# Gate order in the prelude, choice of PSUM banks and load times of the filter slices in a spectral + GeGLU kernel

## Chip, cores and metric

The kernel runs on one core of one Trainium2 chip. The metric is device time in microseconds (us) of one execution, as the median over repeated runs. Five engines work side by side, each through its own queue of instructions in order: TensorE (PE; its weight loads are shown apart as PEld), VectorE (DVE), ScalarE (ACT), GpSimd (POOL) and SyncE (SP). SP, ACT and POOL also issue DMA transfers. Engines wait for each other by semaphores.

## What is computed

The input is layer-normalised, goes through a global spectral filter (two-dimensional real FFT over sequence and features, product with a complex weight, inverse FFT) and through a gated feed-forward layer; both results are added to the input. Sizes: sequence 2048, features 512, feed-forward 1792, bf16 in and out.

```python
xn = _layernorm(x, axis=-1)
# A: spectral filter
X = rfft2(xn.astype(float32), axes=(-2, -1))          # 2048 x 257
y = irfft2(X * (w_r + 1j * w_i), s=(S, D)).astype(bfloat16)
# B: gated feed-forward
h = gelu(xn @ w_gate) * (xn @ w_up)                    # 2048 x 1792
return x + y + h @ w_down
```

## The kernel before

The 2048 rows are 16 row tiles of 128, grouped into 4 blocks `b` of 4 tiles. `xnT` holds the normalised input transposed, so that each 128-row tile is the moving operand of the feed-forward matmuls.

**Feed-forward.** For each block and each of 14 slices `fc` of 128 hidden columns, `gate(b, fc)` runs 4 matmuls on PE (L880) into one PSUM bank, ScalarE applies GELU from the bank into one of three buffers `gl` (L883); `up(b, fc)` runs 4 matmuls (L895) into another bank and VectorE multiplies the two into `hT` (L901). The product with `w_down` is made in a Strassen-like scheme on 7 matmul groups per pair of row tiles: `product(b, p, step)` (L784), with sums of `hT` from VectorE (`sum_01`, L719; `sums_S`, L701) and of `w_down` (`sums_T`, L746). Step 0 is copied between its two banks by ScalarE (L803), and step 1 adds to that copy. Step 2 is the first to read the sums.

**Spectral filter.** It is a chain of small DFT stages on PE, each emptied by ScalarE: a butterfly on VectorE over `xnT` (`butter`, L438 and L439, then L441 and L442), `unit_D` (L455 to L459, evicted by L463), `units_A` (L487 and L490, evicted by L497, then stored to the scratch `scr1` by SP), a reload of the scratch into `tv` (`load_tv`, two loads per block on SP), `unit_B` (L587, evicted by L593, then multiplied on VectorE by the filter slices `wring`, L598), `unit_C` (L612, evicted by L617, stored to `scr2`), `load_vv`, `unit_E` (L640, evicted by L647) and `unit_F` (L838, evicted by L844, then combined and added into the result by a DMA). `unit_B(0)` reads all of `tv`, that is, the loads of all four blocks.

**Layer norm and transposes.** VectorE makes the statistics (`ln_stat`, L385) and the normalised rows (`ln_norm`, L404). Blocks 0 and 1 are transposed on PE (`trans1`, `trans`, L1021 and L414); blocks 2 and 3 by one transposing DMA each on SP's queue (`trans_dma`, L428).

**Order of the work.** Everything is written out by the program in one order; each engine's queue is what that order leaves to it. It begins with a prelude (L1032 to L1061): 12 matmuls on zeros, layer norm of the first tiles one by one, and gates and ups of slices 0 to 5 for the first two tiles of block 0 alone (`T01`), since the first two tiles arrive first. Gates and ups before the main loop may be issued with `ahead`, the number of gates that were issued already and whose `up` isn't yet, so that `gl` buffers aren't mixed up. Then the main loop runs over blocks and slices: gate, `hook()`, up, `hook()`, with products in between. Each `hook()` is a numbered slot; `at(h, ...)` plans calls into slot `h`, in the order in which they were planned. So `at` places the filter chain, the statistics of later blocks and late loads among the feed-forward work.

The slots that matter here: `butter(m, 0)` and `butter(m, 1)` stand in slots `t + 2` and `t + 3` of block `m`'s `t` (L966); `units_A(2)` and `unit_D(12)` in slot 40, `unit_D(13)` to `(15)` in slots 41 to 43; `load_tv(3)` in 48; `sum_01(0, 0, k)` in the slots of L1007; `sums_T(k)` in those of L1009; `unit_B(0)` in 59, `unit_B(1)` in 63, `unit_C(0)` in 64. Slot 28 is the first of block 1.

**Filter slices.** `load_W(s)` makes 8 loads of 64 KB for slice `s`: four of `w_r` on POOL's queue in slots `h0` and `h0 + 1`, then four of `w_i` on SP's queue in `h0 + 2` and `h0 + 3`. `load_late` holds a load back until PE has come to the point of the program where it was planned. The buffer `wring` holds four slices. `keep_256(s)` is a small copy on POOL that waits for slice `s` and must come before slice `s + 4` overwrites it.

**PSUM banks.** There are 8 banks. `take(n, dur, hold)` picks `n` neighbouring banks for the next piece of PE work. It carries a planned PE time `pt`, a planned ScalarE time `act_t` and for each bank the planned time `free` at which it is empty again, and takes the place whose banks are free first; of equals, the lowest:

```python
i = min(range(9 - n), key=lambda i: max(free[i:i + n]))
```

Stages A, B, C and the products take pairs. The plan only chooses the bank; the real order is kept by semaphores, so a PE instruction waits until the bank's last reader is done.

Of the kernel before, what the change touches and what calls it, by code (L numbers as in the profile page):

```python
# [18 lines left out]
P = 128  # L19
# [112 lines left out]
class _Prog:  # L132
# [17 lines left out]
    def op(self, eng, fn, r=(), w=(), dma=False, after=()):  # L150
        deps = [(ev, True) for ev in after]
        for k in r:
            if k in self.writer:
                deps.append((self.writer[k], True))
        for k in w:
            if k in self.writer:
                deps.append((self.writer[k], False))
            for ev in self.readers.get(k, ()):
                deps.append((ev, False))
        need = {}  # L160
        for (st, val), raw in deps:
            if st == eng and not dma and (eng == "pe" or not raw):
                continue
            need[st] = max(need.get(st, 0), val)
        known = self.known[eng]
        need = {s: v for s, v in need.items() if known.get(s, 0) < v}
        need = {s: v for s, v in need.items()
                if not any(s2 != s and self.clk[(s2, v2)].get(s, 0) >= v for s2, v2 in need.items())}
        for s, v in need.items():
            for a, b in self.clk[(s, v)].items():  # L170
                if known.get(a, 0) < b:
                    known[a] = b
        if dma:

            st = None if eng == "pool" else next((d for d in self.dsem if known.get(d, 0) >= self.cnt[d]), None)
            if st is None:
                st = "d%d" % (len(self.sem) - 4)
                self.sem[st] = self.es.enter_context(self.nc.semaphore("s_" + st))
                self.cnt[st] = 0
                if eng != "pool":  # L180
                    self.dsem.append(st)
            self.cnt[st] += 16
            ev, inc = (st, self.cnt[st]), 16
            clk = dict(known)
        else:
            self.cnt[eng] += 1
            ev, inc = (eng, self.cnt[eng]), 1
            clk = dict(self.lastclk[eng])
            for a, b in known.items():
                if clk.get(a, 0) < b:  # L190
                    clk[a] = b
        clk[ev[0]] = ev[1]
        self.clk[ev] = clk
        if not dma:
            self.lastclk[eng] = clk
        self.q[eng].append((fn, list(need.items()), ev[0], inc))
        for k in r:
            self.readers.setdefault(k, []).append(ev)
        for k in w:
            self.writer[k] = ev  # L200
            self.readers[k] = []
        return ev
# [12 lines left out]
def bass_parallel_sum__spectral_gfnet__glu_gated_geglu__prompt_kernel(  # L215
# [27 lines left out]
    with ExitStack() as es:  # L243
        def sb(name, shape, dt):
            return es.enter_context(nc.sbuf_tensor(name, shape, dt))

        pr = _Prog(nc, es)
        op = pr.op

        x_sb = sb("x_sb", [P, NJ, D], BF16)  # L250
        xnT = sb("xnT", [P, NJ, 4, P], F16)
# [5 lines left out]
        wg_sb = sb("wg", [P, 4, FF], BF16)  # L257
# [54 lines left out]
        def bank(i):  # L312
            return psum[:, i * 512:(i + 1) * 512]
# [7 lines left out]
        pt = [0.0]  # L321
        act_t = [0.0]
        free = [0.0] * 8

        def take(n, dur, hold=None, ops=1):
            i = min(range(9 - n), key=lambda i: max(free[i:i + n]))
            pt[0] += dur
            if hold is None:
                act_t[0] = max(act_t[0], pt[0] + 0.25) + 0.2 + 0.43 * n
                end = act_t[0]  # L330
            else:
                end = pt[0] + hold
            for k in range(i, i + n):
                free[k] = end
            return i
# [48 lines left out]
        def ln_stat(j):  # L384
            op("dve", lambda e: e.bn_stats(st[:, j, :], x_sb[:, j, :]), r=[("x", j, 0), ("x", j, 1)], w=[("st", j)])  # L385
# [482 lines left out]

        gun = [0]

        def gate(b, fc, jjs=(0, 1, 2, 3), ahead=0):
            k = gun[0] + ahead
            n = len(jjs) * P
            j0 = 4 * b + jjs[0]
            bg = take(1, 0.0017 * n)

            def fn(e):
                ins = None
                for dc in range(4):
                    ins = e.matmul(bank(bg)[:, 0:n], wg_sb[:, dc, fc * P:(fc + 1) * P], xnT[:, j0:j0 + len(jjs), dc, :], start=(dc == 0), stop=(dc == 3))  # L880
                return ins
            op("pe", fn, r=[("wg", fc)] + [("xnT", b, dc, jj) for dc in range(4) for jj in jjs], w=[("ps", bg)])
            op("act", lambda e: e.activation(gl[k % 3][:, 0:n], bank(bg)[:, 0:n], ACT.Gelu_apprx_tanh), r=[("ps", bg)], w=[("gl", k % 3)])  # L883

        def up(b, fc, jjs=(0, 1, 2, 3), wait=False):
# [49 lines left out]
        def at(h, *calls):  # L935
            plan.setdefault(int(h), []).extend(calls)
# [14 lines left out]
            at(10 + 2 * i, (load_late, wd_sb[:, f0:f1, :], wdv[:, f0:f1, :], [("wd", fc) for fc in range(f0, f1)]))  # L951
        at(18, (load_late, be[:], c_be.ap(), ["be"]))
        at(19, (load_late, mm[:], c_mm.ap(), ["mm"]))
        for s, h0 in enumerate((24, 31, 37, 53, 61, 66, 70, 75)):
            for i, t in enumerate(load_W(s)):
                at(h0 + i // 2, t)
            at(89 + s // 2 if s > 3 else (47, 48, 51, 58)[s], (keep_256, s))
        cmv = c_cm.ap().rearrange("p (h r c) -> p h r c", h=NJ, r=2)
        for i, h0 in enumerate((54, 57, 63, 68)):
            hs = slice(4 * i, 4 * i + 4)  # L960
# [2 lines left out]
        for m in range(1, 4):  # L963
            a = (5, 15, 22)[m - 1]
            n = (10, 20, 27)[m - 1]
            t = (16, 29, 36)[m - 1]  # L966
            for i in range(4):
                at(a + i, (ln_stat, 4 * m + i))
            at(a + 3, (ln_aggr, 4 * m, 4))
            for i in range(4):  # L970
                at(n + i // 2, (ln_norm, 4 * m + i))
            if m < 2:
                at(t, (trans, m, (0, 1), (0, 1, 2, 3)))
                at(t + 1, (trans, m, (2, 3), (0, 1, 2, 3), "act"))
            else:
                at(n + 1, (trans_dma, m))
            at(t + 2, (butter, m, 0))
            at(t + 3, (butter, m, 1))
        at(3, (butter, 0, 0))
        at(4, (butter, 0, 1))  # L980
        for m in range(4):
            h = (11, 22, 35, 40)[m]
# [6 lines left out]
        for g in range(9):  # L989
            h = int(59 + 4.6 * g)  # L990
# [13 lines left out]
            at(107 + 2.2 * j, (unit_E, j))  # L1004
            at(110.5 + 2.2 * j, (unit_F, j))
        for k in range(3):
            at((36, 37, 38)[k], (sum_01, 0, 0, k))  # L1007
        for k in range(4):
            at((39, 43, 45, 47)[k], (sums_T, k))  # L1009
        for k in range(4):  # L1010
            at((101, 101, 102, 103)[k], (sums_S, 2, 0, 4, (k,)))
            at((106, 106, 107, 107)[k], (sums_S, 2, 4, 6, (k,)))
# [27 lines left out]
        ln_norm(1)  # L1040
        trans1(1, ("dve", "act"))
        T01 = (0, 1)
        gate(0, 0, T01)
        ln_stat(2)
        ln_stat(3)
        ln_aggr(2, 2)
        up(0, 0, T01)
        gate(0, 1, T01)
        up(0, 1, T01)
        gate(0, 2, T01)  # L1050
        ln_norm(2)
        ln_norm(3)
        up(0, 2, T01)
        gate(0, 3, T01)
        gate(0, 4, T01, 1)
        up(0, 3, T01)
        up(0, 4, T01)
        trans(0, (0, 1), (2, 3), "dve")
        trans(0, (2, 3), (2, 3), "act")
        gate(0, 5, T01)  # L1060
        up(0, 5, T01)  # L1061
        S3 = {7: [(0, 4, (0,))], 8: [(0, 4, (1,))], 9: [(0, 4, (2,))], 10: [(0, 4, (3,))], 11: [(4, 6, (0, 1))], 12: [(4, 6, (2, 3))],
              13: [(6, 7, (0, 1, 2, 3))]}
# [3 lines left out]
        for b in range(4):  # L1067
            for n, fc in enumerate(range(NFC) if b < 2 else [7 * (i % 2) + i // 2 for i in range(NFC)]):
                jjs = (2, 3) if b == 0 and fc < NH else (0, 1, 2, 3)
# [70 lines left out]
```

## Time and profile before

| | us |
|---|---|
| median of 11 runs | 182.17 (181.15 to 185.1) |
| the profiled execution | 183.22 |
| its span, first to last instruction | 181.4 |

Groups of instructions with most busy time, by line:

| line | engine | what | count | busy us | mean ns |
|---|---|---|---|---|---|
| L880 | PE | gate | 248 | 58.4 | 359 |
| L895 | PE | up | 248 | 58.4 | 359 |
| L901 | DVE | product of gate and up | 62 | 39.3 | 637 |
| L883 | ACT | GELU | 62 | 34.4 | 556 |
| L784 | PE | product with wd, hT | 112 | 14.4 | 273 |
| L598 | DVE | filter product | 16 | 10.3 | 687 |

Matmuls are pipelined, so the mean of one is longer than its distance to the next: four gate matmuls of 512 columns take 0.86 us in a row on the chain of waits. DMA moved 27.89 MB, 154 GB/s in the mean over the span; the mean busy share of the 16 DMA engines, in 40 slices of the span, in tenths:

```profile
DMA  3999999699999566488763121384155755642104
```

A row of a timeline gives the start in us from the span's start, the duration, engine, line, operation, output and inputs, count, and in brackets how long the engine sat idle before it and which instruction released it. "A waits" rows give total, times and longest. SPq and POOLq stand for the issue of DMAs.

### The profile page before, as it was taken

To read this page: it belongs to the slowest core of one execution; us is meant where nothing else is said; L and a number is where in the kernel's file an instruction comes from. 1 tells how busy PE (TensorE), PEld (TensorE's weight loads), DVE (VectorE), ACT (ScalarE), POOL (GpSimd) and SP (SyncE) were. 2 spreads that over 40 slices of the span, in tenths; PEclk is the share of its full clock that TensorE was granted. 3 is DMA by queue.
4 is the path that set the end of the run, shared out by engine and by line. 5 is a ranking of instruction groups with operands and counts; after the bars stand their busy time and mean duration, and the time that the engine had idled before them with its cause. 6 is when DMAs were issued, how large, how long until landed. Compare 5 with 4: busy or idle time off the path is not lost.

```text
span 181.4 us, 3822 instructions
## 1 busy us (share of the span) xinstructions
PE 172.8 (95%) x1406; PEld 108.2 (60%) x1406; DVE 132.8 (73%) x331; ACT 94.0 (52%) x158; POOL 53.5 (29%) x107
## 2 busy tenths in 40 slices
PE   7879999999987999999999999999999999999992
PEld 2468655554546566556655556556676767666882
DVE  3486989987665776776876649797877777897552
ACT  3335547765576632465655755336858677632110
POOL 2210081373250206276470000001354625640000
PEclk9999999999999999999999999999999999999999
DMA  3999999699999566488763121384155755642104
GB/s 97 308 261 305 318 264 317 179 205 186 255 185 155 152 177 175 103 187 192 221 174 90 58 61 58 109 245 171 20 98 105 130 114 102 106 73 43 33 2 116
DMA packets 31059, 27.89 MB, mean 154 GB/s; under 512 B 7120, under 2 KB 27984, under 8 KB 30912
## 3 DMA queue, kind: packets, MB, share of 16 engines
q1 hardware_dynamic: 26016, 19.88, 45.0%
q0 software_dynamic: 4272, 7.24, 18.6%
q10 hardware_dynamic: 752, 0.52, 1.1%
q8 instruction: 11, 0.18, 0.4%
q14 instruction: 8, 0.07, 0.1%
HBM read 18.19 MB, written 6.29 MB: 135 GB/s over the span
## 4 chain that ended last, share of the span: by engine, by line
PE 80%; DMA 8%; DVE 6%; SPq 2%; issue 2%; ACT 1%; DVEq 0%
PE ps L784 24%; PE ps L895 23%; PE ps L880 22%; DMA wu<-in_B_w_up_dram 4%; DMA xnT<-cmx 4%; SPq L338 2%; PE ps L612 2%; PE ps L838 2%; PE ps L640 2%; PE ps L587 2%; DVE st L385 1%; DVE hT L901 1%; DVE cmx L404 1%; PE ps L458 1%; PE ps L459 1%
## 5 line engine op out<-in xcount | busy, mean ns | idle before, releaser
L895 PE MATMUL ps<-xnT,wu 128*128 128x512 f16 (+1 forms) x248 | 58.4, 359 | 1.1 <-DMA wu<-in_B_w_up_dram 1.1
L880 PE MATMUL ps<-xnT,wg 128*128 128x512 f16 (+1 forms) x248 | 58.4, 359 | 0.5 <-ACT xnT L1030 0.5
L901 DVE TENSOR_TENSOR hT<-ps,gl 128x512 bf16<-128x512 f32 (+1 forms) x62 | 39.3, 637 | 21.7 <-PE ps L895 15.4
L883 ACT ACTIVATE gl<-ps 128x512 bf16<-128x512 f32 (+1 forms) x62 | 34.4, 556 | 37.5 <-PE ps L880 34.9
L895 PEld LDWEIGHTS ps<-xnT,wu 128*128 128x128 bf16 x248 | 23.3, 98 | 20.6 <-DMA wu<-in_B_w_up_dram 1.3
L880 PEld LDWEIGHTS ps<-xnT,wg 128*128 128x128 bf16 x248 | 23.3, 98 | 16.1 <-issue 1.4
L341 POOL DMA_DIRECT2D wring<-in_A_w_r_dram x32 | 18.5, 609 | 22.6 <-PE ps L784 9.4
L649 POOL COPY tv<-tv 1x128 bf16<-1x128 bf16 x16 | 5.4, 340 | 42.0 <-ACT tv L647 41.9
L784 PE MATMUL ps<-wd,hT 128*128 128x256 bf16 x112 | 14.4, 273 | 0.0
L864 POOL DMA_DIRECT2D x_sb<-tv x16 | 13.2, 865 | 3.4 <-DVE tv L857 2.4
L385 DVE BATCH_NORM_STATS2 st<-x_sb 128x6 f32<-128x512 bf16 x16 | 10.6, 685 | 3.9 <-DMA x_sb<-in_A_x_dram 3.9
L598 DVE TENSOR_TENSOR early<-early,wring 128x1024 bf16<-128x1024 f16 x16 | 10.3, 687 | 3.8 <-ACT early L593 3.8
L803 ACT ACTIVATE ps<-ps 128x256 f32<-128x256 f32 x16 | 5.9, 369 | 13.1 <-PE ps L784 13.0
L463 ACT ACTIVATE early<-ps 128x512 f16<-128x512 f32 x16 | 9.5, 596 | 5.4 <-PE ps L459 5.4
L784 PEld LDWEIGHTS ps<-wd,hT 128*128 128x128 bf16 x112 | 10.7, 98 | 2.5
L784 PE MATMUL ps<-arena,xnT 128*128 128x256 f16 x91 | 11.4, 273 | 0.0
L844 ACT ACTIVATE tv<-ps 128x512 bf16<-128x512 f32 x16 | 9.5, 595 | 3.6 <-PE ps L838 3.6
L393 POOL TENSOR_TENSOR rstd<-vpe,mhalf 128x4 f32<-128x4 f32 (+2 forms) x6 | 5.0, 837 | 21.5 <-DVE vpe L392 21.5
L647 ACT ACTIVATE tv<-ps 128x512 bf16<-128x512 f32 x16 | 9.5, 596 | 3.2 <-PE ps L640 3.2
L593 ACT ACTIVATE early<-ps 128x1024 f16<-128x1024 f32 x8 | 8.2, 1023 | 4.8 <-PE ps L587 4.8
L784 PEld LDWEIGHTS ps<-arena,xnT 128*128 128x128 f16 x91 | 8.5, 98 | 2.3 <-DVE tw L807 0.3
L667 DVE TENSOR_TENSOR x_sb<-ps,x_sb 128x256 bf16<-128x256 f32 x16 | 6.7, 421 | 3.3 <-PE ps L784 3.2
(119 smaller groups left out, 235.7 us busy)
## 6 DMA issues: line engine op xcount, KB each, us to landing
wring<-in_A_w_r_dram POOLq DMA_DIRECT2D x32, 64.2 KB, 3.6
wring<-in_A_w_i_dram SPq DMA_DIRECT2D x32, 64.2 KB, 3.9
tv<-scr SPq DMA_DIRECT2D x8, 256.0 KB, 4.7
scr<-early SPq DMA_DIRECT2D x8, 256.0 KB, 2.2
wring<-scr SPq DMA_DIRECT2D x4, 512.0 KB, 7.9
x_sb<-tv POOLq DMA_DIRECT2D x16, 128.0 KB, 2.7
scr<-early SPq DMA_DIRECT2D x15, 128.0 KB, 3.6
out_dram<-x_sb SPq DMA_DIRECT2D x28, 64.0 KB, 2.0
```

What stands on the lines that cost most here:

```text
L341: op(eng, lambda e: e.dma_start(dst, src), w=list(keys) + list(also), dma=True, after=[("pe", pr.cnt["pe"])])
L385: op("dve", lambda e: e.bn_stats(st[:, j, :], x_sb[:, j, :]), r=[("x", j, 0), ("x", j, 1)], w=[("st", j)])
L463: op("act", lambda e: e.activation(x4.rearrange("p (a c r) -> p a c r", a=2, r=4), bank(bk).rearrange("p (a r c) -> p a c r", a=2, r=4), A ...
L598: op("dve", lambda e, k=k: e.tensor_tensor(pp[i][k], xc[i], W[k][g % 4][:, :, :, 0:256], ALU.mult), r=[("xc", i)] + [key for c in range(2) ...
L647: op("act", lambda e: e.activation(z, bank(bk).rearrange("p (a c) -> p a c", a=4), ACT.Copy, scale=SC_E), r=[("ps", bk)], w=[zk] + (TVK if ...
L784: ins = e.matmul(o, st_(f), mv(f), start=(f == 0 and step in (0, 5)), stop=(f == 6), skip_group_check=True)
L844: op("act", lambda e: e.activation(o2, bank(bk), ACT.Copy), r=[("ps", bk)], w=[ok] + (TVK if j < 2 else []))
L864: op("pool", lambda e: e.dma_start(x_sb[:, j, :], ys, accum_op=ALU.add), r=[yk + (0,), yk + (1,), ("x", j, 0), ("x", j, 1)] + acc(j), w=ac ...
L880: ins = e.matmul(bank(bg)[:, 0:n], wg_sb[:, dc, fc * P:(fc + 1) * P], xnT[:, j0:j0 + len(jjs), dc, :], start=(dc == 0), stop=(dc == 3))
L883: op("act", lambda e: e.activation(gl[k % 3][:, 0:n], bank(bg)[:, 0:n], ACT.Gelu_apprx_tanh), r=[("ps", bg)], w=[("gl", k % 3)])
L895: ins = e.matmul(bank(bu)[:, 0:n], wu_sb[:, dc, fc * P:(fc + 1) * P], xnT[:, j0:j0 + len(jjs), dc, :], start=(dc == 0), stop=(dc == 3))
L901: op("dve", lambda e: e.tensor_tensor(hT[b % 2][:, fc, h0:h0 + n], bank(bu)[:, 0:n], gl[k % 3][:, 0:n], ALU.mult), r=[("ps", bu), ("gl", k ...
```

## The change

Five edits, with no change to what is computed.

1. In the prelude, the first gate is issued tile by tile: eight matmuls of 128 columns in two groups that each need one tile's `xnT`, into the same bank, evicted by one ScalarE operation as before.
2. The prelude's order: gates 0, 1, 2 are issued ahead of ups 0, 1, 2, and gates 3, 4, 5 ahead of up 3; the transposes of tiles 2 and 3 (`trans`) come after up 3 instead of after up 4.
3. `take` ranks places by three numbers in turn: how long until the place's banks are free, counted from now; how soon two neighbouring pairs that don't overlap would be free if this place were taken; and the old number.
4. Filter slices: `load_W(0)`, `(1)`, `(2)`, `(3)` start in slots 30, 37, 49, 54 instead of 24, 31, 37, 53; `keep_256(2)` in slot 57 instead of 51.
5. Block 3's `t` is 35 instead of 36, so its butterfly stands in slots 37 and 38 instead of 38 and 39; `sum_01(0, 0, k)` in slots 38, 39, 40 instead of 36, 37, 38, and `sums_T(0)` in 40 instead of 39.

```diff
         def take(n, dur, hold=None, ops=1):
-            i = min(range(9 - n), key=lambda i: max(free[i:i + n]))
+            def cost(i):
+
+                fr = [max(0.0, f - pt[0]) for f in free]
+                own = max(fr[i:i + n])
+                fr[i:i + n] = [own + 1.5] * n
+                ps = [max(fr[k:k + 2]) for k in range(7)]
+                return own, min(ps[k] + ps[m] for k in range(5) for m in range(k + 2, 7)), max(free[i:i + n])
+
+            i = min(range(9 - n), key=cost)
...
-        def gate(b, fc, jjs=(0, 1, 2, 3), ahead=0):
+        def gate(b, fc, jjs=(0, 1, 2, 3), ahead=0, split=False):
             k = gun[0] + ahead
             n = len(jjs) * P
-            j0 = 4 * b + jjs[0]
             bg = take(1, 0.0017 * n)
 
-            def fn(e):
-                ins = None
-                for dc in range(4):
-                    ins = e.matmul(bank(bg)[:, 0:n], wg_sb[:, dc, fc * P:(fc + 1) * P], xnT[:, j0:j0 + len(jjs), dc, :], start=(dc == 0), stop=(dc == 3))
-                return ins
-            op("pe", fn, r=[("wg", fc)] + [("xnT", b, dc, jj) for dc in range(4) for jj in jjs], w=[("ps", bg)])
+            for h in (jjs,) if not split else [(jj,) for jj in jjs]:
+                j1, c = 4 * b + h[0], slice(P * (h[0] - jjs[0]), P * (h[-1] - jjs[0]) + P)
+
+                def fn(e, h=h, j1=j1, c=c):
+                    ins = None
+                    for dc in range(4):
+                        ins = e.matmul(bank(bg)[:, c], wg_sb[:, dc, fc * P:(fc + 1) * P], xnT[:, j1:j1 + len(h), dc, :], start=(dc == 0), stop=(dc == 3),
+                                       skip_group_check=split)
+                    return ins
+                op("pe", fn, r=[("wg", fc)] + [("xnT", b, dc, jj) for dc in range(4) for jj in h], w=[("ps", bg)])
             op("act", lambda e: e.activation(gl[k % 3][:, 0:n], bank(bg)[:, 0:n], ACT.Gelu_apprx_tanh), r=[("ps", bg)], w=[("gl", k % 3)])
...
-        for s, h0 in enumerate((24, 31, 37, 53, 61, 66, 70, 75)):
+        for s, h0 in enumerate((30, 37, 49, 54, 61, 66, 70, 75)):
             for i, t in enumerate(load_W(s)):
                 at(h0 + i // 2, t)
-            at(89 + s // 2 if s > 3 else (47, 48, 51, 58)[s], (keep_256, s))
+            at(89 + s // 2 if s > 3 else (47, 48, 57, 58)[s], (keep_256, s))
...
-            t = (16, 29, 36)[m - 1]
+            t = (16, 29, 35)[m - 1]
...
         for k in range(3):
-            at((36, 37, 38)[k], (sum_01, 0, 0, k))
+            at((38, 39, 40)[k], (sum_01, 0, 0, k))
         for k in range(4):
-            at((39, 43, 45, 47)[k], (sums_T, k))
+            at((40, 43, 45, 47)[k], (sums_T, k))
...
         T01 = (0, 1)
-        gate(0, 0, T01)
+        gate(0, 0, T01, 0, True)
+        gate(0, 1, T01, 1)
+        gate(0, 2, T01, 2)
         ln_stat(2)
         ln_stat(3)
         ln_aggr(2, 2)
         up(0, 0, T01)
-        gate(0, 1, T01)
         up(0, 1, T01)
-        gate(0, 2, T01)
+        up(0, 2, T01)
         ln_norm(2)
         ln_norm(3)
-        up(0, 2, T01)
         gate(0, 3, T01)
         gate(0, 4, T01, 1)
+        gate(0, 5, T01, 2)
         up(0, 3, T01)
-        up(0, 4, T01)
         trans(0, (0, 1), (2, 3), "dve")
         trans(0, (2, 3), (2, 3), "act")
-        gate(0, 5, T01)
+        up(0, 4, T01)
         up(0, 5, T01)
```

On the engines, the number of matmuls grows by four (1406 to 1410, the split gate's), with the same columns; all other counts stay. On VectorE the butterfly of block 3 moves ahead of the three `sum_01`. On SP, the four `w_i` loads of slice 0 move from ahead of the second transposing DMA to behind it, and slice 2's four from ahead of the stores of `units_A(2)` to behind `load_tv(3)`. On POOL, slice 0 moves behind the last layer-norm operation, and slice 2 behind the first two `keep_256`.

## The prediction

> **What bounds the kernel now.** I read the page first (busy time, slices, granted clock), then TensorE's waits, then the order of time around each wait, last the DMA issues. The page:
>
> ```profile
> span 181.4 us, 3822 instructions
> PE 172.8 (95%) x1406; PEld 108.2 (60%) x1406; DVE 132.8 (73%) x331; ACT 94.0 (52%) x158; POOL 53.5 (29%) x107
> PEclk9999999999999999999999999999999999999999
> ```
>
> TensorE (PE) is busy 95% of the span at the full granted clock, and the change neither adds nor removes a column of matmul work. So it can win only where PE stands still, and lose only where it makes PE stand still. PE's waits (total, times, longest):
>
> ```profile
> PE ps L455 <- DVE arena L442: 1.7, 1, 1.7
> PE ps L380 <- DVE dumm L350: 1.2, 1, 1.2
> PE ps L895 <- DMA wu<-in_B_w_up_dram: 1.1, 1, 1.1
> PE ps L880 <- ACT xnT L1030: 0.5, 1, 0.5
> PE ps L612 <- ACT early L593: 0.3, 1, 0.3
> ```
>
> Apart from the launch wait (L380) that is 3.6 us, 2% of the span: the ceiling. About 3 us after PE's last matmul are untouched. The longest wait, in order of time:
>
> ```profile
> 45.24 2.99 SPq L428 DMA_TRANSPOSE xnT<-cmx  x1
> ...
> 52.15 0.69 DVE L438 TENSOR_TENSOR cmx<-xnT 128x1024 f16<-128x1024 f16 x1 [1.37 <-DMA xnT<-cmx]
> ...
> 53.36 0.69 DVE L719 TENSOR_TENSOR xnT<-hT 128x512 f16<-128x512 bf16 x2
> 53.97 0.68 DVE L901 TENSOR_TENSOR hT<-ps,gl 128x512 bf16<-128x512 f32 x1
> 54.57 0.41 DVE L441 TENSOR_TENSOR arena<-cmx 128x512 f16<-128x512 f16 x1
> 54.90 0.42 DVE L442 TENSOR_TENSOR arena<-cmx 128x512 f16<-128x512 f16 x1
> ...
> 55.38 0.23 PE L455 MATMUL ps<-fd,arena 128*128 128x128 f16 x1 [1.69 <-DVE arena L442]
> ```
>
> The reader should see two causes: the transposing DMA of the last row block is issued at 45.24 and lands 6.9 us later (its median in the DMA table), and VectorE then puts three other operations between the butterfly's halves (L439, L441).
>
> **Part by part** (minus is time gained).
>
> *Prelude.* `up` of slice 3 waits until 12.31 for the second slice of `w_up`, whose place in SP's queue is unchanged. Before, gates 0 to 4 stand ahead of that wait; after, gates 0 to 5. Moved out from behind it: four 128x256 matmuls, 0.44 on the chain: **-0.44**. The transposes now follow one `up` (0.44) after 12.31 instead of two, at 12.75; their inputs (L404) ended at 12.25, and one product more (0.38) now precedes them on VectorE: 12.63, still in time. ScalarE evicts gates 3 to 5 while PE waits. Bounds: 0 if `w_up` lands later by as much, -0.6 if the 0.07 gap behind goes too.
> Tile by tile, gate 0 is eight matmuls of 128 columns instead of four of 256. The 128-column transposes (L414) take 0.45 for eight, so 0.44 stays 0.44; the first half starts up to 0.5 sooner, and both drown in the wait for `w_up`: 0.
> The Trainium skill (TensorE: Matmul & The Clock Gate, Back-to-back issue gap) speaks against splitting: about 81 ns for each 128-column matmul in a stream with weight loads. By that figure eight would cost an estimated 0.65, 0.2 more, and the sum would still be the same, as `w_up` covers it; the trace's 56 ns decides.
>
> *Filter slices later, butterfly earlier.* Before the transpose, SP issues four loads of `w_i` (39.91 to 42.52) and four stores of `scr`. Slice 0's loads now come after the transpose, so the stores issue as soon as stage A's evictions (39.66 to 41.60) allow: two from 40.6, two to about 42.9, and the transpose at 42.9 instead of 45.24. With 6.9 to 7.6 (the other transpose's row) it lands at 49.8 to 50.5. VectorE reaches the butterfly, now ahead of the sums, after the product at 49.49 to 50.18; spaced as in the rows (0.6, 0.6, 0.33, 0.42), L442 ends by 52.5. PE wants it when stage A ends, 53.5. So the 1.7 wait goes, with 1 us to spare: **-1.7**. The sums (three times 0.6 to 0.7) are late next, wanted at 61.9 by product step 2; the last of them, `sums_T` 1, ended 60.4, and VectorE's total before it is unchanged: 0. PE's next need is the L803 copy behind stage A's two evictions on ScalarE: 55.23 plus 0.5 (L463) plus 0.37, about 56.1; PE would be there 2.6 after 53.5, at 56.1: 0, with 0.3 as bound. If the transpose lands no sooner (52.13, only 0.44 earlier with the prelude), L442 ends at 53.6 against PE at 53.1: -1.15. Bounds of this part: -1.85 (the start-to-start gap) to -0.6.
>
> *Banks.* The first stage C matmul waits for the eviction of the unit B just before, since they share a bank:
>
> ```profile
> 77.91 1.02 ACT L593 ACTIVATE early<-ps 128x1024 f16<-128x1024 f32 x1 [0.62 <-PE ps L587]
> ...
> 79.08 0.63 PE L612 MATMUL ps<-early,cmx 64*64 64x256 bf16 x16 [0.35 <-ACT early L593]
> ```
>
> With the new rule, worked through the planner's calls, that pair is free: **-0.35** (0 to -0.4). But the rule ranks banks by planned, not real, release, and puts gate 11 of block 0 into bank 7, last read by the product of `up` 9:
>
> ```profile
> 31.85 0.69 DVE L901 TENSOR_TENSOR hT<-ps,gl 128x512 bf16<-128x512 f32 x1
> ...
> 32.17 1.03 PE L880 MATMUL ps<-xnT,wg 128*128 128x512 f16 x4
> ...
> 33.26 0.23 PE L455 MATMUL ps<-fd,arena 128*128 128x128 f16 x1
> ```
>
> PE waits from 32.17 to 32.6; the gate (0.86) then ends at 33.46, and the 0.2 wait before L455, which follows, is swallowed: **+0.2** (0 to +0.6, if VectorE doesn't move with PE's 0.44). Queued behind are a `unit_D` and `up` 11.
> In the last third (units E and F) eight gates and one `up` now take a bank whose ScalarE eviction ended 0.18 to 0.19 before PE came; between 124 and 146 every gate and `up` had 1.9 or more. At 79.08 PE started 0.15 after the eviction ended, so 0.04 is left: 0, bound +0.6 (nine times 0.07).
>
> *What the later slices meet.* PE reaches unit B (73.64) some 1.9 sooner. It needs all of `tv`; the last two loads are issued at 67.66 and 68.22 and the trace has them landing at 71.16 and 72.88: 0.76 to spare. Their chain (stage A, eviction, store, load) starts from PE and moves with it. New in that stretch are four `w_r` loads on POOL's queue (from 65.6, after product step 3), before the stores have landed; four `w_i` follow `tv` on SP's queue. Four such loads landed 0.34 apart (73.21 to 74.22), so they can hold `tv` up by 0 to 1.4; half, 0.7, would just use up the spare. SP may also issue the stores later than PE moves: **+0.3** (0 to +1.4). `keep_256` and the `cm` loads queued behind on POOL aren't wanted before 79.
> The Trainium skill (DMA: Bandwidth & Descriptors, Issuing engines are not separate DMA queues) says that loads of all queues share the same 16 engines and interleave, which speaks against putting slices beside `tv`. Nothing in the sum rests on it.
>
> **Sum.** -0.44 - 1.7 - 0.35 + 0.2 + 0.3 = -2.0. Span 181.4 to 179.4, the profiled execution 183.22 to 181.2; that execution is 1.05 over the median of the runs, so I take the difference to the median: 182.17 - 2.0 = **180.2**. Own range, not all bounds met at once: 179.3 to 181.2.
>
> **Rivals.** *The wait moves to unit B.* If `tv` stays bound by SP and the DMA engines (busy over 80% from 36 to 59), it lands at 72.88 as before while PE is there at 71.7: +1.2 instead of +0.3, 181.1; with the four loads' 1.4 in front, 182.4; middle 181.7. For it: 0.76 is little. Against: eight slice loads have left the queue before 49, and the DMA engines are 62% busy from 64 to 73.5.
> *Slower: the tight banks in the last third.* If a 0.37 copy (L803) or the like gets in front of each of the nine evictions, each costs 0.33, 3.0 together: 183.2. It decides only from about 2.9 in all, so all nine must miss. For it: 0.04 is little and repeats. Against: ScalarE is idle before most of these evictions, and gaps of the same 0.14 to 0.20 in the last 12 us show no PE stall.
> *The order doesn't do what it says:* the transpose lands no sooner: 180.7, inside my own range.
>
> **How the numbers follow.** Forecast 0.72, unit B rival 0.15, tight banks 0.08, 0.05 for what I don't see. Some 0.5% (0.9 us) is what a measurement can tell here. Faster: 0.70 of the first, 0.06 of the second, 0.02: 0.78. Same: 0.02, 0.08, 0.01: 0.11. Slower 0.11. The range reaches to the middle of the second case and past: 179.2 to 182.2.
>
> **What would show it.** Right: L455's wait on L442 gone, the second transpose issued over 2 us sooner, L612's wait gone, one new wait of L880 on L901 near 32, and at most half a microsecond of waiting on `tv` by L587. Wrong: L438 still idle for the DMA, a `tv` wait over 1 us, or waits of L880 and L895 on L647 and L844 after 113.

## The result, and the profile after

The changed kernel took 180.87 us (median of 12 runs, 180.3 to 181.97); the kernel before, over the 47 runs there are by then, 182.85 (181.15 to 188.08). The ratio of the two is 0.9912, 95% interval 0.9887 to 0.9937: 0.88% or 1.6 us of 182.17, faster by more than the 0.9 us that can be told from nothing. The ratio is that of the means without executions over 1.5% longer than their kernel's fastest (ten of the 47, none of the 12), so it shows less than the 1.98 us between the medians. The forecast was 2.0 us. The profiled execution of the changed kernel took 180.35 us, 2.87 less than that of before; most of this document is about why the two profiles differ by more than the timed runs.

The page after, its first line and TensorE's busy time:

```profile
span 178.5 us, 3831 instructions
PE 173.2 (97%) x1410; PEld 108.3 (61%) x1410; DVE 132.7 (74%) x331; ACT 93.7 (52%) x158; POOL 54.1 (30%) x107
```

TensorE's waits after (engine, line, what it waited for: total us, times, longest). Lines have moved: 890 is the gate's matmul (880 before), 906 the up's (895), 422 the transposes (414), 412 the normalised rows (404), 463 `unit_D` (455), 450 the last butterfly operation (442), 912 the product on VectorE (901), 595 unit B (587), 620 unit C (612).

```profile
PE ps L388 <- DVE dumm L358: 1.2, 1, 1.2
PE ps L906 <- DMA wu<-in_B_w_up_dram: 0.3, 1, 0.3
PE ps L890 <- DVE hT L912: 0.3, 1, 0.3
PE ps L422 <- DVE cmx L412: 0.3, 1, 0.3
```

The 1.7 us wait of `unit_D` and unit C's 0.3 are gone. The wait for `w_up` is 0.3 where it was 1.1. One wait is new: a gate (L890) waits for VectorE's product (L912). The last row is an old one, 0.25 us in both profiles. The order of time (start, duration, engine, line, operation) around the places that the prediction named:

```profile
11.71 0.61 PE L906 MATMUL ps<-xnT,wu 128*128 128x256 f16 x4 [0.27 <-DMA wu<-in_B_w_up_dram]
12.31 0.62 PE L422 MATMUL ps<-ident,cmx 128*128 128x128 f16 x8
...
30.98 0.69 DVE L912 TENSOR_TENSOR hT<-ps,gl 128x512 bf16<-128x512 f32 x1
...
31.73 1.04 PE L890 MATMUL ps<-xnT,wg 128*128 128x512 f16 x4 [0.26 <-DVE hT L912]
...
32.60 0.22 PE L463 MATMUL ps<-fd,arena 128*128 128x128 f16 x1
...
42.71 2.02 SPq L436 DMA_TRANSPOSE xnT<-cmx  x1
...
50.33 0.69 DVE L446 TENSOR_TENSOR cmx<-xnT 128x1024 f16<-128x1024 f16 x1 [0.82 <-DMA xnT<-cmx]
50.94 0.68 DVE L447 TENSOR_TENSOR arena<-xnT 128x1024 f16<-128x1024 f16 x1
51.54 0.42 DVE L449 TENSOR_TENSOR arena<-cmx 128x512 f16<-128x512 f16 x1
51.88 0.42 DVE L450 TENSOR_TENSOR arena<-cmx 128x512 f16<-128x512 f16 x1
...
52.95 0.23 PE L463 MATMUL ps<-fd,arena 128*128 128x128 f16 x1
...
71.21 0.41 PE L595 MATMUL ps<-tv,be 64*64 64x256 f16 x8
...
75.48 1.02 ACT L601 ACTIVATE early<-ps 128x1024 f16<-128x1024 f32 x1 [0.62 <-PE ps L595]
...
76.23 0.63 PE L620 MATMUL ps<-early,cmx 64*64 64x256 bf16 x16
```

The first two rows stood so before:

```profile
12.31 1.05 PE L895 MATMUL ps<-xnT,wu 128*128 128x256 f16 x8 [1.06 <-DMA wu<-in_B_w_up_dram]
...
13.19 0.50 PE L414 MATMUL ps<-ident,cmx 128*128 128x128 f16 x6
```

The second transposing DMA is issued 2.5 us sooner (42.71, before 45.24); its four VectorE operations follow without a stranger between them, and `unit_D` starts 0.65 after the last of them has ended (52.30). The row at 71.21 is unit B(0), which doesn't wait. Unit C starts while the eviction of the unit B before it is still running: it has other banks.

The same matmul in both traces gives the gain step by step (start after minus start before): `up` of slice 3 -0.60; the transposes behind it -0.88; `unit_D(4)` -0.66; `unit_D(12)` -2.43; unit C(0) -2.85; the end -2.85. The -0.60 is odd: nothing ahead of that `up`'s data changed. The second `w_up` transfer simply landed at 11.66 instead of 12.26.

That gives a measure for all runs below: the span less the start of the prelude's transposes. It leaves the landing of `w_up` out. It is 181.4 - 13.19 = 168.2 before and 178.55 - 12.31 = 166.2 after: **2.0 us** are won behind the prelude.

### The profile page after: what moved, and what is told of

It is laid out like the page before. It is cut to its first block, busy times and chain, and to the rows that moved or that the text cites. A ratio compares the mean times of both kernels' runs of the same rounds, so it can differ in the third digit from the quotient of the medians.

```text
span 178.5 us, 3831 instructions
## 1 busy us (share of the span) xinstructions
PE 173.2 (97%) x1410; PEld 108.3 (61%) x1410; DVE 132.7 (74%) x331; ACT 93.7 (52%) x158; POOL 54.1 (30%) x107
## 4 chain that ended last, share of the span: by engine, by line
PE 82%; DVE 7%; DMA 4%; SPq 2%; issue 2%; POOL 1%; ACT 0%; DVEq 0%
PE ps L792 24%; PE ps L906 23%; PE ps L890 23%; DMA wu<-in_B_w_up_dram 4%; DVE st L393 3%; SPq L346 2%; PE ps L620 2%; PE ps L648 2%; PE ps L846 2%; PE ps L595 2%; DVE hT L912 2%; PE ps L495 1%; PE ps L466 1%; PE ps L498 1%; PE ps L467 1%
## 5 line engine op out<-in xcount | busy, mean ns | idle before, releaser
L890 PE MATMUL ps<-xnT,wg 128*128 128x512 f16 (+2 forms) x252 | 58.1, 355 | 0.4 <-DVE hT L912 0.3
L906 PE MATMUL ps<-xnT,wu 128*128 128x512 f16 (+1 forms) x248 | 58.1, 359 | 0.3 <-DMA wu<-in_B_w_up_dram 0.3
L912 DVE TENSOR_TENSOR hT<-ps,gl 128x512 bf16<-128x512 f32 (+1 forms) x62 | 39.2, 636 | 20.4 <-PE ps L906 14.4
L906 PEld LDWEIGHTS ps<-xnT,wu 128*128 128x128 bf16 x248 | 23.3, 98 | 19.8 <-issue 1.0
L890 PEld LDWEIGHTS ps<-xnT,wg 128*128 128x128 bf16 x252 | 23.3, 98 | 16.4 <-issue 1.4
```

The lines of the kernel that those rows point to most:

```text
L890: ins = e.matmul(bank(bg)[:, c], wg_sb[:, dc, fc * P:(fc + 1) * P], xnT[:, j1:j1 + len(h), dc, :], start=(dc == 0), stop=(dc == 3), skip_g ...
L906: ins = e.matmul(bank(bu)[:, 0:n], wu_sb[:, dc, fc * P:(fc + 1) * P], xnT[:, j0:j0 + len(jjs), dc, :], start=(dc == 0), stop=(dc == 3))
L912: op("dve", lambda e: e.tensor_tensor(hT[b % 2][:, fc, h0:h0 + n], bank(bu)[:, 0:n], gl[k % 3][:, 0:n], ALU.mult), r=[("ps", bu), ("gl", k ...
```

## The experiments

Every row is one profiled execution; "to the end" is the measure just named, and the last two columns are timed runs against the kernel before on the same chip. The first row of the changed kernel is the result above; the others come from three later sets of timed runs, each with its own runs of the kernel before. The second set (the changed kernel again, slices only, butterfly only, slice 2 at 44) is on another chip than the first and the third.

| kernel | `w_up` lands | transposes start | to the end | wait at `unit_D(12)` | wait at unit B(0) | ratio | interval |
|---|---|---|---|---|---|---|---|
| before | 12.26 | 13.19 | 168.2 | 1.86 | 0 | | |
| changed | 11.66 | 12.31 | 166.2 | 0 | 0 | 0.9912 | 0.9887-0.9937 |
| changed, again | 11.35 | 12.14 | 166.2 | 0 | 0 | 0.9845 | 0.979-0.9899 |
| prelude only | 11.91 | 12.55 | 168.7 | 1.32 | 0 | 1.0057 | 1.001-1.0104 |
| bank rule only | 12.76 | 13.69 | 168.5 | 2.40 | 0 | 1.0005 | 0.9957-1.0053 |
| slices and butterfly only | 12.11 | 13.04 | 166.8 | 0 | 0.41 | 0.9932 | 0.9897-0.9967 |
| slices only | 12.77 | 13.70 | 167.2 | 0.39 | 0.53 | 0.9971 | 0.9932-1.001 |
| butterfly only | 11.17 | 12.40 | 166.8 | 0.39 | 0 | 0.9897 | 0.9834-0.996 |
| changed, old bank rule | 12.81 | 13.30 | 168.6 | 0 | 1.28 | 0.9979 | 0.9937-1.0021 |
| changed, first gate whole | 12.51 | 13.00 | 166.2 | 0 | 0 | 0.9863 | 0.9812-0.9914 |
| changed, slice 2 at 44 | 12.86 | 13.36 | 167.7 | 0 | 1.54 | 0.9872 | 0.9812-0.9933 |
| changed, slices 2, 3 at 52, 56 | 12.56 | 13.05 | 166.2 | 0 | 0 | 0.9898 | 0.9856-0.994 |
| changed, statistics later | 12.52 | 13.02 | 165.5 | 0.18 | 0 | 0.9826 | 0.9775-0.9876 |
| changed, both of the last two | 12.82 | 13.31 | 165.4 | 0 | 0 | 0.9863 | 0.9809-0.9916 |

Waits in this table are gaps between two matmuls' starts less the first one's time (0.11), so they are 0.1 to 0.2 longer than the page's. Where nothing was waited for, the same measure gives 0.09 (0.20 from start to start), which the table shows as 0; so what a wait costs is its entry less 0.09, 1.77 for 1.86.

**1. The prelude alone**: the new order of gates and ups, and the split first gate; the rest as before.

```diff
-        gate(0, 0, T01)
+        gate(0, 0, T01, 0, True)
+        gate(0, 1, T01, 1)
+        gate(0, 2, T01, 2)
...
         gate(0, 4, T01, 1)
+        gate(0, 5, T01, 2)
         up(0, 3, T01)
```

> Only the prelude's new order and the split first gate; old bank rule, old slots of slices and butterfly. Theory (the parts' prices are those of the two traces, and the bank rule is needed by the new order): the prelude gives -0.44 us at its gate and +0.16 at the transposes, so about -0.3 us up to product 25; the L442 wait at unit D(12) stays at some 1.8 us; and since the old bank rule now starts from another place, the wait of unit C(0) goes (-0.45) but unit C(3), near 91 us, gets a pair that an eviction on ACT still holds, about 1.2 us. Sum: +0.3 us, 0 to +0.5. Rival A (the prelude is worth the 0.88 us that the traces differ by at the transposes, and banks play no part): 0.6 to 0.9 us faster, with no wait at unit C(3). Rival B (the 0.60 us at up(0,3) is an accident of when w_up lands): in this profile that up can stand anywhere between 11.7 and 12.3 us, whatever the order on PE.

Measured: 0.57% slower (1.0 us). The order of time shows where it goes:

```profile
91.36 1.02 ACT L593 ACTIVATE early<-ps 128x1024 f16<-128x1024 f32 x1 [0.62 <-PE ps L587]
...
92.53 0.63 PE L612 MATMUL ps<-early,cmx 64*64 64x256 bf16 x16 [1.22 <-ACT early L593]
```

Unit C(3) stands still for the whole eviction of unit B that was queued just before it, since the old rule gave both the same pair of banks. Nothing in the prelude's edit touches that place: the planner counts on from an earlier clock and runs into a bad pair 80 us later. In the traces the kernel needs 0.5 more to the end and starts the transposes 0.3 sooner after the landing, +0.2 together where +0.3 was expected; the timed runs say more, with an interval from 0.1 to 1.0%. The profiled execution was the shortest of its 12 (183.03, median 184.13), and its wait at `unit_D(12)` 0.54 shorter than in the profile of before: its transposing DMA landed 38.4 after the transposes (38.9 before). Rival A falls: the prelude is not worth 0.88. Rival B stands: `w_up` landed at 11.91.

**2. The bank rule alone** (`key=cost` in `take`, everything else as before).

> Only the new bank rule. Theory: unit C(0)'s wait goes, -0.42 us; gate(0,11) waits some 0.45 us for bank 7, which takes the place of the 0.2 to 0.26 us wait at unit D(4) and delays the late L442 wait's counterpart by nothing, +0.2; unit D(12)'s wait stays at about 1.7 us, being set by a landing. Sum -0.2 to -0.5 us, which the timing can hardly tell from nothing. Rival (bank choice alone carries a good part of the gain): -1 us or more, with unit D(12)'s wait shortened.

Measured: no difference (1.0005). Unit C(0)'s wait is gone and gate 11's is there (0.43), as expected. What I had not expected is a longer wait of `unit_D(12)`; the profile's DMA issues (size left out, us to landing) and TensorE's row:

```profile
xnT<-cmx SPq DMA_TRANSPOSE x1, 8.4
```
```profile
56.62 0.23 PE L463 MATMUL ps<-fd,arena 128*128 128x128 f16 x1 [2.24 <-DVE arena L450]
```

The transposing DMA took 8.4 us, 1.5 more than in the profile of before, with the same transfers around it. As long as `unit_D(12)` hangs on that landing, its wait differs between executions: 1.32, 1.86 and 2.40 in the three traces with the old slots.

**3. Slices and butterfly, together and apart.** Together:

```diff
-        for s, h0 in enumerate((24, 31, 37, 53, 61, 66, 70, 75)):
+        for s, h0 in enumerate((30, 37, 49, 54, 61, 66, 70, 75)):
-            at(89 + s // 2 if s > 3 else (47, 48, 51, 58)[s], (keep_256, s))
+            at(89 + s // 2 if s > 3 else (47, 48, 57, 58)[s], (keep_256, s))
-            t = (16, 29, 36)[m - 1]
+            t = (16, 29, 35)[m - 1]
-            at((36, 37, 38)[k], (sum_01, 0, 0, k))
+            at((38, 39, 40)[k], (sum_01, 0, 0, k))
-            at((39, 43, 45, 47)[k], (sums_T, k))
+            at((40, 43, 45, 47)[k], (sums_T, k))
```

The first two changes are the slices, the last three the butterfly.

> Only the later slices and the earlier butterfly; prelude and bank rule as before. Theory: the wait of unit D(12) on L442 goes whole, -1.77 us; nothing at unit B(0), as in the changed kernel; unit C(0)'s 0.45 us wait stays. Sum -1.8 us (-1.3 if unit B(0) does wait, by 0.47). Rival (the parts only work together): less than 1 us, with a wait of a new tile in the place of unit D(12)'s.

> Only the later slices. Theory: they free the way of the transposing DMA of block 3, which lands as early as in the run with both parts, but sum_01 still stands ahead of L442 in DVE's order: unit D(12) waits 0.3 to 0.7 us, so 1.0 to 1.4 us faster than before less what unit B(0) waits in its profile (0 to 1.3). Rival (the slices are nothing, the butterfly's place is all): unit D(12) waits 1.2 us or more.

> Only the earlier butterfly and the later sums. Theory: the transposing DMA is issued no earlier than before, since the slice transfers still stand ahead of it on SP, and lands at 51 to 53 us; L442 starts right after it, so unit D(12)'s wait shrinks by 0.5 to 1.2 us, and unit B(0), with the slices where they were, does not wait. 0.5 to 1.2 us faster than before. Rival (slices alone decide): unit D(12) still waits 1.5 us or more.

Measured: 0.68% (1.2 us), 0.29% (0.5 us, not told from nothing) and 1.03% (1.9 us) faster. Both together remove the wait of `unit_D(12)` whole; unit B(0) waits, and the 1.4 us less to the end are near the -1.3 given for that case. Each alone leaves 0.39 of the wait. VectorE and TensorE with the slices alone:

```profile
52.41 0.68 DVE L719 TENSOR_TENSOR xnT<-hT 128x512 f16<-128x512 bf16 x2
53.02 0.68 DVE L901 TENSOR_TENSOR hT<-ps,gl 128x512 bf16<-128x512 f32 x1
53.62 0.41 DVE L441 TENSOR_TENSOR arena<-cmx 128x512 f16<-128x512 f16 x1
53.95 0.41 DVE L442 TENSOR_TENSOR arena<-cmx 128x512 f16<-128x512 f16 x1
...
54.42 0.23 PE L455 MATMUL ps<-fd,arena 128*128 128x128 f16 x1 [0.23 <-DVE arena L442]
```

Here the DMA has landed (50.92) before VectorE gets to it, but a sum and a product stand between the butterfly's halves. With the butterfly alone it is the other way round:

```profile
51.10 0.69 DVE L438 TENSOR_TENSOR cmx<-xnT 128x1024 f16<-128x1024 f16 x1 [1.71 <-DMA xnT<-cmx]
...
52.65 0.41 DVE L442 TENSOR_TENSOR arena<-cmx 128x512 f16<-128x512 f16 x1
...
53.12 0.23 PE L455 MATMUL ps<-fd,arena 128*128 128x128 f16 x1 [0.23 <-DVE arena L442]
```

VectorE idles 1.71 us for the landing and then runs the four operations in one go. So either half is worth some 1.46 (1.86 - 0.39) and both 1.77: they overlap. My expectation for the butterfly alone (0.5 to 1.2 off the wait) was too low. From the landing to L442's end it took 3.19 before (55.32 - 52.13) and 1.98 here (53.06 - 51.08), so the order alone is worth 1.2; the other 0.26 is the landing, 38.94 after the prelude's transposes before and 38.68 here.

The slices' price is in the next column of the table: unit B(0) waits 0.41 and 0.53 where they are late, nothing with the butterfly alone. The row with the slices alone:

```profile
73.13 0.41 PE L587 MATMUL ps<-tv,be 64*64 64x256 f16 x8 [0.37 <-DVE xnT L719]
```

The row names a VectorE sum, but the last `tv` load is what it waits for: unit B(0) starts 0.24 after that landing here (72.89) and with both parts (71.81, start 72.05), as it does in the two kernels below whose rows name the DMA. So both together and the butterfly alone need the same 166.8 us to the end: in these traces the slices won 0.30 at `unit_D(12)` and gave 0.32 back at unit B(0).

**4. The changed kernel with the old bank rule.**

> The changed kernel with the old bank rule. Theory: the new order with the old rule puts unit C(3), near 90 us, on a pair that an ACT eviction holds: a wait of 1.2 us; gate(0,11)'s 0.43 us goes and unit D(4)'s 0.26 us returns; sum about +1.0 us against the changed kernel, so 0.6 to 1.0 us faster than before. Rival (bank choice is worth what it was predicted at, -0.15 us net): within 0.3 us of the changed kernel.

Measured: 0.21% (0.4 us) faster than before, not told from nothing, and 2.4 us longer "to the end" than the changed kernel, where 1.0 was expected. Two waits make up most of that:

```profile
73.18 0.41 PE L587 MATMUL ps<-tv,be 64*64 64x256 f16 x8 [1.12 <-DMA tv<-scr]
```
```profile
93.23 0.52 PE L612 MATMUL ps<-early,cmx 64*64 64x256 bf16 x12 [1.22 <-ACT early L593]
```

The second is unit C(3) again, as expected, so with the new prelude the bank rule is worth about 1.1 us: 1.29 at unit C(3), from start to start, less the 0.21 of gate 11. The first was not in the expectation and is the prediction's rival at unit B(0): the last `tv` load was issued at 66.51 and landed at 72.94, 6.4 us, where it took 4.9 in the changed kernel. This execution was the second longest of its 12 (183.76, median 181.92), so most of the others needn't have had that wait.

**5. The changed kernel once more.**

> The changed kernel once more, to see what differs between two executions of it. Theory (two transfers set how long an execution is, the second w_up slice at up(0,3) and the tv(3) loads at unit B(0)): w_up lands anywhere between 11.6 and 12.8 us and moves the later work with it; unit B(0) waits 0 to 1.3 us, more where the tv(3) loads take more than the 4.6 and 4.9 us of the first profile. The gate(0,11) wait of 0.43 and the transposes' 0.42 us at product 24 are there again to within 0.02. Timed 1.5 to 2.0 us faster than before. Rival (the first profile was typical, and the kernel before varies alone): w_up at 11.7, no wait at unit B(0), and the timed runs 2.5 us faster than before.

Measured: 1.55% (2.8 us) faster, interval 1.0 to 2.1%, and a second profile that agrees with the first in every wait behind the prelude (0.42 and 0.43 in the middle, "to the end" 166.2). `w_up` landed at 11.35, and the transposes then waited 0.31 for VectorE's normalisation (L412). Unit B(0) did not wait: its data had landed at 70.72, it started at 71.05. So more was gained than expected (1.5 to 2.0 us), and the rival's 2.5 us and its unit B(0) without a wait come nearer. A wait there is not in every execution of the late slices, and both profiles of the changed kernel were taken in executions with an early `w_up`.

**6. The split of the first gate**: the changed kernel with `gate(0, 0, T01)`.

> The changed kernel with the first gate in one piece. Theory (what stands ahead of up(0,3) only shortens or lengthens that up's wait for w_up): where w_up lands at 11.6 us or later, the transposes start where they start in the changed kernel, 0.49 to 0.65 us after the landing, and nothing is lost; timed within 0.3 us of it. Rival (the split is worth its 0.2 to 0.5 us at the first gate): the transposes start 0.2 us or more later against the landing than in the changed kernel, and the time is longer by that.

Measured: "to the end" the same, the transposes 0.49 after the landing of `w_up`, as in the other late landings of the new order. Nothing is lost in the trace. The split's eight matmuls of 128 columns in the changed kernel start 55 to 56 ns apart within each half. No runs of the changed kernel stand in the same set, so the expected 0.3 us between the two times can't be read closely (180.77 here, 180.70 and 180.87 there).

**7. Slices away from `tv`.** The changed kernel with slice 2 due at 44, ahead of the `tv` loads:

```diff
-        for s, h0 in enumerate((30, 37, 49, 54, 61, 66, 70, 75)):
+        for s, h0 in enumerate((30, 37, 44, 54, 61, 66, 70, 75)):
```

> The changed kernel with one number changed: filter slice 2 due at step 44, not 49, so that its four POOL transfers are issued at about 57.5 us, after the last transposing DMA has landed (50.3) and ahead of the tv(3) loads (65.2). Theory (slice 2 beside tv(3) is what unit B(0) waits for in some executions): the tv(3) loads land in 3.5 to 4.7 us, as before the change, unit B(0) never waits, and the timed runs are 0.3 to 0.6 us faster than the changed kernel's and scatter less. Rival (tv(3) is late for other reasons, or the slice now delays the scr(3) stores): the same time as the changed kernel to within 0.3 us, or slower.

A miss: unit B(0) waited longest of all.

```profile
61.34 1.94 SPq L346 DMA_DIRECT2D scr<-early  x3
63.33 3.03 SPq L349 DMA_DIRECT2D wring<-in_A_w_i_dram  x4
67.07 2.32 SPq L346 DMA_DIRECT2D tv<-scr  x2
...
73.69 0.41 PE L595 MATMUL ps<-tv,be 64*64 64x256 f16 x8 [1.37 <-DMA tv<-scr]
```

In the changed kernel:

```profile
60.19 1.94 SPq L346 DMA_DIRECT2D scr<-early  x3
65.16 1.15 SPq L346 DMA_DIRECT2D tv<-scr  x2
```

The second `tv` load was issued at 68.80, 55.4 after the transposes (53.4 in the changed kernel). Its own way took 4.65. Slice 2's four `w_i` loads now stand between the last stores and the `tv` loads on SP's queue. The last of these stores landed 4.3 us after its issue (66.94), in the changed kernel 3.5 (65.03), and in both traces the first `tv` load was issued 0.13 after that landing: 0.86 later, counted from the transposes. Its issue then took 1.69 us instead of 0.51. Together that is the 2.0. So the rival's second half, a slice that delays the stores, fits these rows; why the issue took longer isn't shown. This execution was the longest of its six (182.83, the others 180.39 to 181.46), so the others needn't have had a wait of that size. The timed runs, 181.42 against 180.70 us of the changed kernel in the same set, don't tell the two apart. Then both slices later:

```diff
-        for s, h0 in enumerate((30, 37, 49, 54, 61, 66, 70, 75)):
+        for s, h0 in enumerate((30, 37, 52, 56, 61, 66, 70, 75)):
-            at(89 + s // 2 if s > 3 else (47, 48, 57, 58)[s], (keep_256, s))
+            at(89 + s // 2 if s > 3 else (47, 48, 60, 61)[s], (keep_256, s))
```

> The changed kernel with slices 2 and 3 due at 52 and 56, not 49 and 54, so that no slice transfer is issued in the 6 us ahead of tv(3) (their POOL copies at 60 and 61). Theory: tv(3)'s loads take 3.5 to 4.7 us, land before 70 us (plus what w_up is late), unit B(0) never waits, 0.3 to 0.6 us faster than the changed kernel and less scatter. What would speak against it: slice 2 or 3 landing after the multiplications that need them, a new wait of unit C(1) to C(3), or the POOL copies holding later slices. Rival (what makes tv(3) late is not the slices): unit B(0) waits as before, same time to within 0.3 us.

The rival holds as to the time: 166.2 to the end, like the changed kernel, and no faster. The last `tv` load took 4.5 us; over the six traces of the new bank rule with slices 2 and 3 at 49 and 54 or later it was 4.0 to 5.0, and unit B(0) never waited. The three in which it took 5.7 to 6.4 all have the late slices and the old bank rule. Whether the rule has to do with it or three accidents met is open.

**8. A faster version: VectorE's queue in the middle.** The two waits that the change left, both on VectorE: block 2's statistics two steps later, block 1's transposes one step later.

```diff
-            a = (5, 15, 22)[m - 1]
+            a = (5, 17, 22)[m - 1]
-            t = (16, 29, 35)[m - 1]
+            t = (17, 29, 35)[m - 1]
```

> The changed kernel with block 1's transposes one step later (17, not 16) and block 2's statistics two steps later (17, not 15) on DVE. Theory (the two waits left in the middle, 0.42 us of the transposes on L412 near 24.5 and 0.43 us of gate(0,11) on DVE's product near 31.6, are both DVE running late): both go, a wait of some 0.2 us at unit D(8) comes, 0.5 to 0.7 us faster than the changed kernel where w_up and tv(3) land alike, which the timed runs show as 0.2 to 0.8 us. Rival (unit B(0) waits for a landing anyway, so that what is won before it is lost there): the two waits go, unit B(0) waits longer by the same, and the time stays within 0.2 us.

> Both of the two edits before it. Theory: the gains add, 0.6 to 1.2 us faster than the changed kernel, since the earlier end of the middle no longer runs into tv(3). Rival (they are the same gain, met twice): no better than the better of the two.

TensorE's waits with the first edit:

```profile
PE ps L388 <- DVE dumm L358: 1.2, 1, 1.2
PE ps L906 <- DMA wu<-in_B_w_up_dram: 0.7, 1, 0.7
PE ps L890 <- ACT xnT L1041: 0.2, 1, 0.2
PE ps L1032 <- DVE cmx L412: 0.2, 1, 0.2
```

Both waits in the middle are gone; 0.09 came at `unit_D(12)` (0.18 in the table) instead of the expected 0.2 at `unit_D(8)`. To the end 165.5, 0.75 less than the changed kernel (0.42 + 0.43 - 0.09 is 0.76), and 180.32 us timed (179.22 to 180.77): 1.74% (3.2 us) faster than before, the fastest of the study by the timed runs. The interval overlaps with that of the changed kernel with its first gate whole, timed in the same set (0.9863), so the 0.75 rests on the traces. The two edits together: 165.4, no better than the better of the two; the rival holds.

## Why the prediction was right, point by point

**The forecast** was -2.0 us, 180.2; the median is 180.87 and the difference by ratio 1.6 (2.8 when the changed kernel was timed again). The ceiling of 3.6 us left out two rows of 0.2 us each in the list of waits before (L414 and L1021 on L404), so it was 4.0. The sum, against the traces:

| term | predicted | shown |
|---|---|---|
| prelude, four matmuls out from behind `w_up` | -0.44 | -0.44 where `w_up` lands from 12.5 on, -0.26 to -0.29 earlier |
| split first gate | 0 | 0 |
| `unit_D(12)` on the butterfly | -1.7 | -1.77 |
| unit C(0)'s bank | -0.35 | -0.42 |
| gate 11 in bank 7, less the wait it swallows | +0.2 | +0.21 |
| nine tight banks in the last third | 0 | 0 |
| unit B(0) beside the late slices | +0.3 | 0 |
| sum | -2.0 | -2.2 to -2.4 |

**Prelude.** The old order starts the transposes 0.93 after the landing (13.19 - 12.26; again 0.93 in the traces with 12.11, 12.76 and 12.77). The new order starts them 0.49 to 0.50 after it in the six traces that land at 12.5 or later: 0.44 less, the price of the step. The 0.88 between the two first profiles is 0.60 of landing and 0.28 of order. The step "12.63, still in time" was wrong in the number: the product more starts earlier and fills idle time of VectorE, and the transposes' inputs (L412) ended at 12.26, where they ended at 12.25 before. They are in time only with a late landing. At 11.66 the transposes waited 0.16 for L412, and at 11.35 0.31; the old order cannot start before 12.40 either (11.17), which leaves 0.26 (12.40 - 12.14).

**Slices and butterfly.** The transposing DMA was issued at 42.71 (predicted 42.9), landed at 50.31 (49.8 to 50.5), L450 ended at 52.30 (by 52.5), and TensorE was there at 52.95; the spare was 0.65, not 1: the 53.5 at which TensorE was to come left out what the prelude gains. The sums that were "late next" cost nothing, and no wait on the copy behind stage A appeared.

**Banks.** Both new and lost waits came where and about as large as they were worked out. What the sum could not show is that the rule's price depends on the other edits: with the old order nothing that the timed runs can tell, with the new prelude about 1.1 us in the traces, since unit C(3) otherwise shares a pair. My term of -0.15 was the price of the assignment that results, not of the edit.

**Unit B.** The term that was off most. The +0.3 stood between 0 and 1.4; the changed kernel showed 0 twice (spare 0.1 to 0.3), and other kernels with the same late slices 0.41, 0.53 and 1.28. The rival "the wait moves to unit B" did not happen in the changed kernel's traces, though its mechanism exists. The 0.76 "to spare" before was counted to the landing; with the 0.24 from landing to start it was 0.52.

**Luck in the sum.** Without the +0.3 the forecast would have been -2.3, as the traces of the changed kernel have it. The -2.0 lies nearer to the timed 1.6 because of a term that these traces don't show; whether other executions had that wait isn't known.

**The rivals.** The tight banks made no wait at any of the nine places (none of L890 or L906 on an eviction among the waits, and the 2.85 gained at unit C(0) is still 2.85 at the end). "The order doesn't do what it says" is refuted by the issue 2.5 us sooner.

**The timed difference.** The two first profiles differ by 2.85, of which 0.60 was when `w_up` landed. The rest, 2.2 to 2.4, lies above the interval of the first timed result (1.6 with 1.1 to 2.1) and inside that of the second (2.8 with 1.8 to 3.8). What the executions that were not profiled waited for isn't known; that their `w_up` landed later, or that unit B(0) waited in some, would both bring the first result down. The long executions of the kernel before, up to 188 us, are explained in part: the landings seen account for about 2.4 us (1.3 where the transposes start, 12.40 to 13.70, and 1.1 in the wait of 1.32 to 2.40), and many had a lower granted clock (last section).

## What to carry to other kernels

Before two traces are compared, look for the first instruction whose shift can't come from the edit; here it was a weight load's landing, worth 0.6 of 2.85 us, and a measure that starts behind it (2.0 us, the same in two executions) gave the parts their size. A planner that hands out PSUM banks turns any edit ahead of it into an edit of every bank behind it, so price the resulting assignment, and test edits of order and of the planner together as well as apart. A load that is moved out of the way of one transfer can come into the way of another that this one waits for: slice 2, taken away from `tv`, came between the stores and the `tv` loads, and in the execution profiled unit B(0) waited 1.5 us where it had not waited.

## What the runs showed of the hardware

The same early transfer, with the same queue ahead of it, landed between 11.17 and 12.86 us in 14 executions. The second transposing DMA (block 3's) took 6.8 to 8.4 us from issue to landing; the first one, block 2's, of the same size, took 4.4 to 5.0 us wherever slice 0 was late, and 7.2 to 7.6 in three of four traces with slice 0's loads beside it (5.4 in the fourth). The Trainium skill (DMA: Bandwidth & Descriptors, Issuing engines are not separate DMA queues) says that transfers of all queues interleave on the same engines; the row of the 7.2 to 7.6 agrees with it.

The mean granted clock of TensorE was 0.981 to 0.991 in 21 of the 94 timed executions, in the three later sets, of the kernels that keep the old slots of slices and butterfly (before, prelude only, bank rule only), and each of these 21 took 184.29 us or more. In the 96 timed executions of all other kernels it was never below 0.997. What lowers it isn't shown, as no trace was taken of such an execution.
